# Attention stage: r loaded two tokens to a partition and spread by ScalarE, r's scaling and the conversion's clamp given new places in the step

## The chip, the cores and the metric

The kernel runs on one core of a Trainium2 chip. The metric is the device time of one execution in microseconds (us), lower is better. Before the change it is 455.89 us, the median of three runs that lie between 454.84 and 456.10 us.

## The reference

Three layers follow each other. Every array of the attention layer is float32; the last layer's arrays are float64.

```python
# r, k, v: [4, 8, 768, 48]; w, u: [8, 48]
state = np.zeros((B, H, D, D), dtype=np.float32)
for t in range(S):
    kt, vt, rt = (k[:, :, t], v[:, :, t], r[:, :, t])
    cur = np.einsum('bhd,bhe->bhde', u[None] * kt, vt)
    y[:, :, t] = np.einsum('bhd,bhde->bhe', rt, state + cur)
    state = w[None, :, :, None] * state + np.einsum('bhd,bhe->bhde', kt, vt)
...
# x = y as [3072, 384]; a soft mixture of 8 experts with 4 slots each
logits = x @ phi
...
# w_in: [384, 2048], w_out: [2048, 384], both float64
h = x @ w_in
g = np.where(h > 0.0, h, alpha * (np.exp(np.minimum(h, 0.0)) - 1.0))
return (g @ w_out).astype(np.float32)
```

## The kernel before

The attention layer is done in chunks of 128 tokens: 4 sequences of 6 chunks, 24 chunks in all, and one pass of the loop `for s in range(-2, NCH)` (lines 857 and after) is called a step here. A step works on several chunks at once, so that each engine has something of a later chunk to do while another chunk is waiting. In step s the kernel finishes the output rows of chunk s, makes the masked scores of chunk s + 1, and prepares r and k of chunk s + 2.

For a chunk these things happen:

- `load_r`, `load_k`, `load_v` (lines 502 to 514) bring 128 tokens of 8 heads, one token to a partition; a contiguous run in memory is one head's 48 floats, 192 bytes.
- `scale` (L517) multiplies k by powers of w on VectorE and writes `km`, whose heads are padded to 64 columns. r is loaded straight into the padded tiles `rp`.
- `turn(0, n)` transposes r: four transposes on TensorE into the PSUM tile `ps_r` (L522), then VectorE scales it by powers of w into `rT` (L532). `turn(1, n)` does the same for k: `ps_k` (L522), a copy by ScalarE into `kT` (L527), and the product r x k by VectorE, `qd` (L529).
- `update` (`pu`, L541), `scores` (`ps_a`, L554, one PSUM tile for the even and one for the odd heads), `causal` (`am`, L559: the mask on VectorE, one instruction for each of the two tiles), `bonus_a`, `bonus_c`, `bonus_b` (`ps_b`, `bt`, `ps_c`, `bs`, and `bv` on GpSimd, L601), `state` and `state_b` (`t1`, `qc` on GpSimd, `qb` on ScalarE).
- `before` (`py`, L612) starts the output of a chunk from the state, `rows_a` (`py`, L625) adds the scores' part, `rows_b` (`x`, L635) adds the bonus on VectorE and so empties the one PSUM tile `py`. `x_T` transposes the finished rows (`ps_x`, L644) and ScalarE copies them to `xT` (L646).

`ps_r`, `ps_x` and `ps_k` share a PSUM pool of two buffers (tag "pt"), so each of them waits until a buffer's readers are done. The pool chooses the buffer when the program is built.

Beside this, each of the first 20 steps converts a piece of the last layer's float64 weights into float32 ("wide"): two operations on ScalarE (`wide_a`, L313 and L314), a clamp (`wide_b1`, L317), a shift with a mask (`wide_b2`, L322), `wide_b3` (L328) and `wide_c` (L333) on VectorE, and in the following step `wide_d` on GpSimd (L336 and L337). They all work in place on the tile `scr`, in the order a, b1, b2, b3, c, d.

The order on each engine is written by hand: the program runs under `manual_schedule`, engines take their instructions in the order of the Python calls, and semaphores alone decide when each starts. All loads are issued from SyncE's queue, in the order of the calls. After the attention layer come the experts and then the last layer (from about 205 us on); the change touches neither.

Of the kernel before, what the change touches and what calls it, by code (L numbers as in the profile page):

```python
# [8 lines left out]
F32 = mybir.dt.float32  # L9
# [4 lines left out]
ALU = mybir.AluOpType  # L14
# [222 lines left out]
def kernel(  # L237
# [14 lines left out]
    nc = tc.nc  # L252
    B, H, S, D = r.shape
# [4 lines left out]
    C = 128  # L258
# [138 lines left out]
    with ExitStack() as actx:  # L397
# [28 lines left out]
        def tables():  # L426
            nc.vector.tensor_scalar(
                out=wd, in0=w_raw, scalar1=W_LO, scalar2=W_HI, op0=ALU.max, op1=ALU.min
            )

            nc.vector.memset(pw[:, 0, :, 0:1], 1.0)
            nc.vector.tensor_copy(out=pw[:, 0, :, 1:2], in_=wd.unsqueeze(2))
            n = 2
            while n <= 64:
                m = min(n - 1, 65 - n)
                nc.vector.tensor_tensor(
                    out=pw[:, 0, :, n:n + m], in0=pw[:, 0, :, 1:1 + m],
                    in1=pw[:, 0, :, n - 1:n].to_broadcast([128, HP, m]), op=ALU.mult,
                )
                n += m  # L440
            nc.vector.reciprocal(out=ri[:, :, 0:8], in_=pw[:, 0, :, 0:8])
            nc.vector.reciprocal(out=ri[:, :, 8:17], in_=pw[:, 0, :, 0:65:8])
            nc.vector.tensor_tensor(
                out=pw[:, 1, :, 0:64].rearrange("p h (b a) -> p h b a", a=8),
                in0=ri[:, :, 8:16].unsqueeze(3).to_broadcast([128, HP, 8, 8]),
                in1=ri[:, :, 0:8].unsqueeze(2).to_broadcast([128, HP, 8, 8]), op=ALU.mult,
            )
            nc.vector.tensor_copy(out=pw[:, 1, :, 64:65], in_=ri[:, :, 16:17])

            nc.vector.tensor_tensor(  # L450
                out=vt[:, :, 0:64], in0=pw[:, 0, :, 0:64], in1=pw[:, 1, :, 64:65].to_broadcast([128, HP, 64]),
                op=ALU.mult,
            )
            nc.scalar.copy(out=vt[:, :, 64:128], in_=pw[:, 0, :, 0:64])
            nc.vector.tensor_tensor(
                out=vk[:, :, 0:64], in0=pw[:, 1, :, 0:64], in1=pw[:, 0, :, 63:64].to_broadcast([128, HP, 64]),
                op=ALU.mult,
            )
            nc.scalar.copy(out=vk[:, :, 64:128], in_=pw[:, 1, :, 1:65])
            ps = pt_p.tile([128, 512], F32, tag="pt", name="ps_wk")  # L460
            for p in range(HP):
                nc.tensor.transpose(out=ps[:, 128 * p:128 * p + 128], in_=vk[:, p, 0:128], identity=ident)
            nc.scalar.copy(out=wk, in_=ps.rearrange("p (h d) -> p h d", d=64)[:, :, 0:D])
# [25 lines left out]
                    out=i3[32 * g:32 * g + 32, :], in_=ident[32 * g:32 * g + 32, 32 * g:32 * g + 32]  # L489
                )  # L490

        rp = [ae2.tile([128, H, 64], F32, name=f"rp{i}", bufs=1) for i in range(2)]
        km = ae1.tile([128, H, 64], F32, name="km")
        kT = ae1.tile([128, HP, 128], F32, name="kT")
        qb = [at1.tile([128, HP, 2, D], F32, name=f"qb{i}") for i in range(2)]
        t1 = at1.tile([128, HP, D], F32, name="t1")
        qc = at1.tile([128, HP, D], F32, name="qc")

        rk, vd, rT, qd, am, bsb, xs, xT, misc = {}, {}, {}, {}, {}, {}, {}, {}, {}


        def load_r(n):
            b, c = divmod(n, NC)
            nc.sync.dma_start(out=rp[n % 2][:, :, 0:D], in_=r[b, :, C * c:C * c + C, :].rearrange("h p d -> p h d"))

        def load_k(n):
            b, c = divmod(n, NC)
# [8 lines left out]
        def scale(n):  # L516
            nc.vector.tensor_tensor(out=km[:, :, 0:D], in0=rk.pop(n), in1=wk, op=ALU.mult)  # L517

        def turn(i, n):
            ps = pt_p.tile([128, HP, 128], F32, tag="pt", name=f"ps_{'rk'[i]}")  # L520
            for p in range(HP):
                nc.tensor.transpose(  # L522
                    out=ps[:, p, :], in_=(km if i else rp[n % 2])[:, 2 * p:2 * p + 2, :].rearrange("p a d -> p (a d)"),
                    identity=ident,
                )
            if i:
                nc.scalar.copy(out=kT, in_=ps)  # L527
                qd[n] = at2.tile([128, HP, 128], F32, tag="qd", name="qd", bufs=1)
                nc.vector.tensor_tensor(out=qd[n], in0=rT[n], in1=ps, op=ALU.mult)  # L529
            else:  # L530
                rT[n] = at2.tile([128, HP, 128], F32, tag="rT", name="rT", bufs=2)
                nc.vector.tensor_tensor(out=rT[n], in0=ps, in1=vt, op=ALU.mult)  # L532


        pu = pu_p.tile([128, HP, D], F32, name="pu")
        nc.vector.memset(pu, 0.0)
# [16 lines left out]
                q = slice(64 * a, 64 * a + 64)  # L553
                nc.tensor.matmul(out=aps[a][:, p, :], lhsT=kT[q, p, :], rhs=rT[n][q, p, :], start=True, stop=True)  # L554

        def causal(n):
            for a in range(2):
                am[n, a] = at2.tile([128, HP, 128], F32, tag="am", name="am", bufs=3)
                nc.vector.tensor_tensor(  # L559
                    out=am[n, a], in0=aps[a], in1=mask.unsqueeze(1).to_broadcast([128, HP, 128]), op=ALU.mult  # L560
                )

        def bonus_a(n):
            pb = pm_p.tile([128, 512], F32, tag="pm", name="ps_b")
# [20 lines left out]
        def state_b(n):  # L585
            if n % NC < NC - 1:
                for a in range(2):
                    s = slice(64 * a, 64 * a + 64)
                    nc.scalar.copy(out=qb[(n + 1) % 2][s, :, a, :], in_=qc[s])
# [223 lines left out]
        def wide(j, f):  # L813
            if 0 <= j < NP:
                raw, a = piece(j)
                if f is not wide_d:
                    f(raw, a)
                    return
                merged = []
                for o, at, i, c, p, m in spans(j):  # L820
                    if merged and merged[-1][0] == o:
                        merged[-1][3] += m
                    else:
                        merged.append([o, at, p, m])
                for o, at, p, m in merged:
                    wide_d(raw[:, at:at + m, :], a[:, at:at + m], (wov if o else wiv)[:, p:p + m])
# [2 lines left out]
        load_k(0)  # L829
        load_v(0)  # L830
        nc.scalar.dma_start(out=phi_sb, in_=phi.rearrange("(k p) c -> p k c", p=128))
        for t in (*rp, km):
            nc.gpsimd.memset(t[:, :, D:], 0.0)
        nc.gpsimd.memset(uw, 0.0)
        for i in range(2):
# [3 lines left out]
        nc.scalar.activation(out=wf, in_=wf, func=ACTF.Exp)  # L839
        warm(12)  # L840
        tables()
        load_r(1)
        load_k(1)
        load_v(1)
# [9 lines left out]
        for s in range(-2, NCH):  # L854
# [26 lines left out]
            if now:  # L881
                for p in range(HP):
                    rows_a(s, p)
                rows_b(s)
                wide(s, wide_b1)
                wide(s - 1, wide_d)
                if s >= 1 and s + 2 < NP:
                    wide_load(s + 2)
            if nxt:
                for p in range(HP):  # L890
                    scores(s + 1, p)
                causal(s + 1)
                bonus_a(s + 1)
                bonus_c(s + 1)
            if not last:
                extra()
            if ahead:
                turn(0, s + 2)
            if 2 <= s + 4 < NCH:
                load_r(s + 4)  # L900
            if nxt:
                for p in range(HP):
                    before(s + 1, p)
# [3 lines left out]
                logits(GS - 1, G - 1, G)  # L907
            if nxt:
                bonus_b(s + 1)
            wide(s, wide_b2)  # L910
            if ahead:
                turn(1, s + 2)
            wide(s, wide_b3)
            wide(s, wide_c)
            if nxt:
                state_b(s + 1)
            if s == NCH - 2:
                warm(3)
            extra()
# [502 lines left out]
```

## Time and profile before

| | before |
|---|---|
| time, median of 3 runs | 455.89 us |
| the profiled execution's own time | 454.1 us |
| its span, first to last instruction | 452.4 us |
| TensorE busy | 414.1 us, 92% |
| TensorE weight loads busy | 361.4 us, 80% |
| VectorE busy | 369.3 us, 82% |
| ScalarE busy | 262.2 us, 58% |
| GpSimd busy | 157.2 us, 35% |
| granted TensorE clock, mean | 0.995 of full speed |
| loads of r (`rp`) | 24 of 192 KB |

The shares are means over the whole span, and the kernel has stages with different limits. The change lies in the first 170 us, so it is read from the views of that stretch: busy time by windows, waits, and the timelines of single steps.

### The profile page before, as it was taken

To read this page: it belongs to the slowest core of one execution; us is meant where nothing else is said; L and a number is where in the kernel's file an instruction comes from. 1 tells how busy PE (TensorE), PEld (TensorE's weight loads), DVE (VectorE), ACT (ScalarE), POOL (GpSimd) and SP (SyncE) were. 2 spreads that over 40 slices of the span, in tenths; PEclk is the share of its full clock that TensorE was granted. 3 is DMA by queue.
4 is the path that set the end of the run, shared out by engine and by line. 5 is a ranking of instruction groups with operands and counts; after the bars stand their busy time and mean duration, and the time that the engine had idled before them with its cause. 6 is when DMAs were issued, how large, how long until landed. Compare 5 with 4: busy or idle time off the path is not lost.

```text
span 452.4 us, 10086 instructions
## 1 busy us (share of the span) xinstructions
PE 414.1 (92%) x4021; PEld 361.4 (80%) x4021; DVE 369.3 (82%) x581; ACT 262.2 (58%) x482; POOL 157.2 (35%) x170
## 2 busy tenths in 40 slices
PE   6988988898988989997999999998999899999995
PEld 5876776776776874455999999996989889999994
DVE  5899989899898744768889999995989889768661
ACT  2543453545453332337787878874777768776750
POOL 2355455456446413500003333350213135423340
PEclk9999999999999999999999999998999999999999
DMA  8979799999999968940001111111111002011212
GB/s 124 227 163 268 191 258 265 266 282 186 269 266 260 278 212 280 313 175 1 0 1 35 36 35 38 35 36 35 36 35 35 1 0 72 35 54 52 71 71 76
DMA packets 97575, 57.41 MB, mean 127 GB/s; under 512 B 77808, under 2 KB 89328, under 8 KB 97520
## 3 DMA queue, kind: packets, MB, share of 16 engines
q1 hardware_dynamic: 96704, 56.64, 46.0%
q8 instruction: 33, 0.54, 0.5%
q14 instruction: 22, 0.18, 0.1%
q10 hardware_dynamic: 816, 0.05, 0.1%
HBM read 51.96 MB, written 4.72 MB: 125 GB/s over the span
## 4 chain that ended last, share of the span: by engine, by line
PE 54%; DVE 24%; issue 9%; ACT 7%; DMA 3%; SPq 1%; POOL 1%; DVEq 0%; ACTq 0%; POOLq 0%
PE fo L1261 10%; PE fo L1264 10%; PE fo L1262 10%; DVE ex L1235 4%; DVE ex L1230 4%; PE fh L1216 3%; PE py L612 3%; PE ps_k L522 3%; PE ps_a L554 2%; PE pd L1029 2%; PE ph L1007 2%; DVE am L559 2%; PE py L625 2%; DVE km L517 2%; DVE scr L317 2%
## 5 line engine op out<-in xcount | busy, mean ns | idle before, releaser
L1261 PE MATMUL fo<-wh,gh 128*128 128x384 f32 x384 | 130.8, 341 | 3.8 <-ACT acc L1198 2.7
L1262 PE MATMUL fo<-wl,gh 128*128 128x384 f32 x384 | 130.1, 339 | 0.0
L1264 PE MATMUL fo<-wh,gl 128*128 128x384 f32 x384 | 125.9, 340 | 3.3 <-DVE gl L1246 3.3
L1230 DVE SCALAR_TENSOR_TENSOR ex<-ex,th 128x1024 f32<-128x1024 f32 (+1 forms) x52 | 60.9, 1172 | 23.8 <-ACT ex L1227 23.6
L1261 PEld LDWEIGHTS fo<-wh,gh 128*128 128x128 f32 x384 | 72.5, 189 | 8.6 <-ACT acc L1198 4.3
L1264 PEld LDWEIGHTS fo<-wh,gl 128*128 128x128 f32 x384 | 72.0, 188 | 4.2 <-DVE gl L1246 4.2
L1262 PEld LDWEIGHTS fo<-wl,gh 128*128 128x128 f32 x384 | 72.4, 189 | 1.9
L1224 ACT ACTIVATE th<-fh 128x1024 f32<-128x1024 f32 (+1 forms) x53 | 50.4, 951 | 38.0 <-PE fh L1216 38.0
L1246 DVE TENSOR_TENSOR gl<-ex,gh 128x1024 fp32r<-128x1024 f32 (+1 forms) x52 | 68.3, 1314 | 1.7 <-ACT gh L1243 1.3
L336 POOL TENSOR_TENSOR cv<-raw,cv 128x384 f32<-128x384 f32 x12 | 19.4, 1620 | 136.5 <-ACT gh L1243 51.5
L1235 DVE SCALAR_TENSOR_TENSOR ex<-ex,fh 128x1024 f32<-128x1024 f32 (+1 forms) x52 | 58.8, 1131 | 0.5 <-ACT ex L1227 0.4
L1227 ACT ACTIVATE ex<-fh 128x1024 f32<-128x1024 f32 (+1 forms) x53 | 50.3, 949 | 9.7 <-DVE gl L1246 9.5
L1243 ACT CAST gh<-ex 128x1024 fp32r<-128x1024 f32 (+1 forms) x52 | 51.4, 988 | 6.2 <-DVE ex L1235 4.9
L1203 POOL TENSOR_TENSOR acc<-os,acc 128x384 f32<-128x384 f32 x20 | 26.7, 1346 | 44.0 <-ACT os L1202 44.0
L646 ACT COPY xT<-ps_x 128x384 f32<-128x384 f32 x24 | 11.5, 479 | 43.2 <-PE ps_x L644 43.2
L583 POOL TENSOR_TENSOR qc<-t,w 128x192 f32<-128x192 f32 x20 | 14.5, 725 | 59.7 <-DVE t L582 21.8
L1216 PE MATMUL fh<-cT,mst 128*128 128x512 f32 x96 | 31.1, 404 | 1.9 <-DVE mst L1144 1.1
L559 DVE TENSOR_TENSOR am<-ps_a,mask 128x512 f32<-128x512 f32 x48 | 30.7, 678 | 0.2 <-PE ps_a L554 0.2
L529 DVE TENSOR_TENSOR qd<-rT,ps_k 128x512 f32<-128x512 f32 x24 | 16.5, 686 | 15.3 <-ACT kT L527 15.3
L554 PE MATMUL ps_a<-rT,kT 64*128 64x128 f32 x384 | 27.9, 285 | 0.3 <-ACT kT L527 0.2
L522 PE MATMUL ps_k<-ident,km 128*128 128x128 f32 x96 | 15.6, 285 | 12.4 <-ACT xT L646 6.4
L625 PE MATMUL py<-vd,am 128*64 128x48 f32 x768 | 26.5, 222 | 0.0
(161 smaller groups left out, 695.0 us busy)
## 6 DMA issues: line engine op xcount, KB each, us to landing
we<-in_moe_w_dram SPq DMA_DIRECT2D x14, 768.0 KB, 8.0
we<-in_moe_w_dram SPq DMA_DIRECT2D x16, 512.0 KB, 6.2
rp<-in_r_dram SPq DMA_DIRECT2D x24, 192.0 KB, 4.6
rk<-in_k_dram SPq DMA_DIRECT2D x24, 192.0 KB, 4.6
vd<-in_v_dram SPq DMA_DIRECT2D x24, 192.0 KB, 4.8
out_dram<-acc SPq DMA_DIRECT2D x24, 192.0 KB, 1.9
we<-in_moe_w_dram SPq DMA_DIRECT2D x16, 256.0 KB, 5.4
scr<-in_moe_w_out_dram SPq DMA_DIRECT2D x10, 384.0 KB, 5.7
```

The costliest lines, as they stand in the source:

```text
L554: nc.tensor.matmul(out=aps[a][:, p, :], lhsT=kT[q, p, :], rhs=rT[n][q, p, :], start=True, stop=True)
L559: nc.vector.tensor_tensor(out=am[n, a], in0=aps[a], in1=mask.unsqueeze(1).to_broadcast([128, HP, 128]), op=ALU.mult)
L1216: nc.tensor.matmul(out=ph[n][:, i, :], lhsT=mst[(f + i) // 8][:, 128 * ((f + i) % 8):128 * ((f + i) % 8) + 128], rhs=cT[:, TB * blk:TB * b ...
L1224: nc.scalar.activation(out=th[n][:, s], in_=ph[n][:, s], func=ACTF.Tanh, scale=0.5)
L1227: nc.scalar.activation(out=ex[n][:, s], in_=ph[n][:, s], func=ACTF.Exp)
L1230: nc.vector.scalar_tensor_tensor(out=ex[n][:, s], in0=ex[n][:, s], scalar=1.0, in1=th[n][:, s], op0=ALU.add, op1=ALU.mult)
L1235: nc.vector.scalar_tensor_tensor(out=ex[n][:, s], in0=ex[n][:, s], scalar=0.0, in1=ph[n][:, s], op0=ALU.min, op1=ALU.max)
L1243: nc.scalar.copy(out=gh[n][:, s], in_=ex[n][:, s])
L1246: nc.vector.tensor_tensor(out=gl[n][:, s], in0=ex[n][:, s], in1=gh[n][:, s].bitcast(F32), op=ALU.subtract)
L1261: nc.tensor.matmul(out=o, lhsT=gh[n][:, i, s], rhs=wh, start=(f == first), stop=False)
L1262: nc.tensor.matmul(out=o, lhsT=gh[n][:, i, s], rhs=wl, start=False, stop=False)
L1264: nc.tensor.matmul(out=o, lhsT=gl[n][:, i, s], rhs=wh, start=False, stop=(f == final))
```

## The change

r is loaded for two chunks at once into `rw`, with two consecutive tokens to a partition, so that a contiguous run is 384 bytes; there are 12 such loads. `spread` copies on ScalarE the even or the odd tokens of such a pair of chunks into the padded tile `rp`, one copy for each chunk's worth of tokens. `turn_r` transposes them as before, but its scaled result goes to every second column of a tile `rT` for both chunks, so that both halves must have been turned before the first of the two chunks can be used. For that, `turn_r` runs one step earlier than `turn(0, ...)` did; two spreads and one `turn_r` stand ahead of the loop, and the second of these spreads goes into the memory of `kT` (`k0`), since `rp` is one tile now.

Inside a step, `turn_r` with r's scaling stands between the two masking instructions, the clamp b1 goes from behind `x` to just ahead of r x k, and the shift b2 goes behind r x k.

```diff
+            spread(0)
+            spread(1, k0)
             ps = pt_p.tile([128, 512], F32, tag="pt", name="ps_wk")
...
-        rp = [ae2.tile([128, H, 64], F32, name=f"rp{i}", bufs=1) for i in range(2)]
+        rw = [ae2.tile([128, H, 2, D], F32, name=f"rw{i}", bufs=1) for i in range(2)]
+        rp = ae2.tile([128, H, 64], F32, name="rp", bufs=1)
...
-        def load_r(n):
-            b, c = divmod(n, NC)
-            nc.sync.dma_start(out=rp[n % 2][:, :, 0:D], in_=r[b, :, C * c:C * c + C, :].rearrange("h p d -> p h d"))
+        def load_r(g):
+            b, c = divmod(2 * g, NC)
+            nc.sync.dma_start(
+                out=rw[g % 2].rearrange("p h j d -> p h (j d)"),
+                in_=r[b, :, C * c:C * c + 2 * C, :].rearrange("h (p j) d -> p h (j d)", j=2),
+            )
+
+        def spread(i, dst=rp):
+            if i < NCH:
+                nc.scalar.copy(out=dst[:, :, 0:D], in_=rw[i // 2 % 2][:, :, i % 2, :])
...
+        def turn_r(i, src=rp):
+            if i >= NCH:
+                return
+            ps = flip(src, "ps_r")
+            g, j = divmod(i, 2)
+            if j == 0:
+                rg[g] = at2.tile([128, HP, 2 * C], F32, tag="rT", name="rT", bufs=2)
+                for c in range(2):
+                    rT[2 * g + c] = rg[g][:, :, C * c:C * c + C]
+            nc.vector.tensor_tensor(
+                out=rg[g].rearrange("p h (c u j) -> p h c u j", c=2, j=2)[:, :, :, :, j],
+                in0=ps.rearrange("p h (c u) -> p h c u", c=2),
+                in1=vt.rearrange("p h (u j) -> p h u j", j=2)[:, :, :, j].unsqueeze(2).to_broadcast([128, HP, 2, 64]),
+                op=ALU.mult,
+            )
...
         tables()
+        turn_r(0)
         load_r(1)
...
                 rows_b(s)
-                wide(s, wide_b1)
                 wide(s - 1, wide_d)
...
-                causal(s + 1)
+                causal(s + 1, 0)
                 bonus_a(s + 1)
                 bonus_c(s + 1)
             if not last:
                 extra()
-            if ahead:
-                turn(0, s + 2)
-            if 2 <= s + 4 < NCH:
-                load_r(s + 4)
+            turn_r(s + 3, k0 if s == -2 else rp)
+            if nxt:
+                causal(s + 1, 1)
+            if s % 2 == 0 and s // 2 + 3 < NCH // 2:
+                load_r(s // 2 + 3)
...
+            wide(s, wide_b1)
+            if ahead:
+                turn_k(s + 2)
             wide(s, wide_b2)
-            if ahead:
-                turn(1, s + 2)
             wide(s, wide_b3)
             wide(s, wide_c)
             if nxt:
                 state_b(s + 1)
+            spread(s + 4)
```

`flip` holds the four transposes, and `turn_k` is what `turn(1, ...)` was.

In the program as built, VectorE's part of a step reads so before (a middle step, from the output rows `x` to the end of the conversion):

```order
L635 TENSOR_TENSOR x<-py,bv 128x384
L317 TENSOR_SCALAR scr<-scr 128x384
L559 TENSOR_TENSOR am<-ps_a,mask 128x512 x2
L532 TENSOR_TENSOR rT<-ps_r,vt 128x512
L322 TENSOR_SCALAR scr<-scr 128x384
L529 TENSOR_TENSOR qd<-rT,ps_k 128x512
L328 SCALAR_TENSOR_TENSOR scr<-scr 128x384
L333 TENSOR_SCALAR scr<-scr 128x384
```

and so after the change, in the same step:

```order
L658 TENSOR_TENSOR x<-py,bv 128x384
L582 TENSOR_TENSOR am<-ps_a,mask 128x512
L546 TENSOR_TENSOR rT<-ps_r,vt 128x512
L582 TENSOR_TENSOR am<-ps_a,mask 128x512
L317 TENSOR_SCALAR scr<-scr 128x384
L557 TENSOR_TENSOR qd<-rT,ps_k 128x512
L322 TENSOR_SCALAR scr<-scr 128x384
L328 SCALAR_TENSOR_TENSOR scr<-scr 128x384
L333 TENSOR_SCALAR scr<-scr 128x384
```

r's scaling has two instructions ahead of it instead of four; the clamp (L317) stands where the shift (L322) stood, and the shift is behind `qd`.

On TensorE the order within a step is the same, but what the transposes of k wait for is not. Before, in a middle step (the names in brackets are the semaphores of the engines waited for; Activation is ScalarE):

```order
L612 MATMUL py<-qb_147,rT 128x96 [waits DVE_49,Activation_49]
L612 MATMUL py<-qb_147,rT 128x96 x3
L644 MATMUL ps_x<-ident,x 128x128 x3
L594 MATMUL ps_c<-ident,bt 128x128 [waits Activation_49]
L522 MATMUL ps_k<-ident,km 128x128 [waits Activation_49]
```

and after:

```order
L635 MATMUL py<-qb_148,rT 128x96 [waits DVE_49]
L635 MATMUL py<-qb_148,rT 128x96 x3
L667 MATMUL ps_x<-ident,x 128x128 x3
L617 MATMUL ps_c<-ident,bt 128x128 [waits Activation_49]
L532 MATMUL ps_k<-ident,km 128x128 [waits DVE_49]
```

The first transpose of k waited for ScalarE and now waits for VectorE.

At the start, VectorE goes from the last table to the first k (`km`) like this before:

```order
L455 TENSOR_TENSOR vk<-pw 128x4x64
L466 TENSOR_TENSOR w_141<-pw 128x4
L469 TENSOR_TENSOR uw<-ud,wd 64x4 x2
L517 TENSOR_TENSOR km<-rk_155,wk 128x8x48
L532 TENSOR_TENSOR rT<-ps_r,vt 128x512
```

and after:

```order
L455 TENSOR_TENSOR vk<-pw 128x4x64
L546 TENSOR_TENSOR rT<-ps_r,vt 128x512
L468 TENSOR_TENSOR w_141<-pw 128x4
L471 TENSOR_TENSOR uw<-ud,wd 64x4 x2
L527 TENSOR_TENSOR km<-rk_156,wk 128x8x48
L546 TENSOR_TENSOR rT<-ps_r,vt 128x512
```

A scaling of r, which needs r's first transposes, stands ahead of the small tables and of `km`.

## Rows read from the trace of the kernel before

**Rows 1.** Busy time by windows: window, us, PE, PEld, DVE, ACT, POOL, clock, DMA share.

```profile
80.00:90.00 10.00, 8.61 (x167) 7.26 (x162) 9.22 (x19) 5.33 (x17) 3.58 (x5) 1.00 1.02 284
```

**Rows 2.** Waits between 15 and 169 us: total us, times, longest.

```profile
PE ps_k L522 <- ACT xT L646: 6.4, 14, 0.5
PE ps_k L522 <- DVE rT L532: 5.2, 6, 1.3
```

**Rows 3.** VectorE's timeline, two steps: start, us, what, [idle before <- releaser].

```profile
76.38 0.55 DVE L635 TENSOR_TENSOR x<-py,bv 128x384 f32<-128x384 f32 x1
76.85 0.34 DVE L317 TENSOR_SCALAR scr<-scr 128x384 f32<-128x384 f32 x1
77.12 1.28 DVE L559 TENSOR_TENSOR am<-ps_a,mask 128x512 f32<-128x512 f32 x2
...
80.44 0.69 DVE L529 TENSOR_TENSOR qd<-rT,ps_k 128x512 f32<-128x512 f32 x1 [1.06 <-ACT kT L527]
...
83.43 0.54 DVE L635 TENSOR_TENSOR x<-py,bv 128x384 f32<-128x384 f32 x1
83.90 0.70 DVE L317 TENSOR_SCALAR scr<-scr 128x384 f32<-128x384 f32 x1
...
87.49 0.69 DVE L529 TENSOR_TENSOR qd<-rT,ps_k 128x512 f32<-128x512 f32 x1 [0.23 <-ACT kT L527]
```

**Rows 4.** TensorE's timeline in the first of these two steps.

```profile
78.34 0.27 PE L594 MATMUL ps_c<-ident,bt 128*128 128x128 f32 x1
79.08 0.66 PE L522 MATMUL ps_k<-ident,km 128*128 128x128 f32 x4 [0.46 <-ACT xT L646]
```

**Rows 5.** ScalarE's timeline in that step.

```profile
78.54 0.48 ACT L646 COPY xT<-ps_x 128x384 f32<-128x384 f32 x1 [2.46 <-PE ps_x L644]
78.92 0.17 ACT L596 COPY bs<-ps_c 128x8 f32<-128x8 f32 x1
79.82 0.59 ACT L527 COPY kT<-ps_k 128x512 f32<-128x512 f32 x1 [0.73 <-PE ps_k L522]
```

**Rows 6.** TensorE's timeline in step 20, at 151 to 157 us.

```profile
153.25 0.27 PE L594 MATMUL ps_c<-ident,bt 128*128 128x128 f32 x1
153.42 0.66 PE L522 MATMUL ps_k<-ident,km 128*128 128x128 f32 x4
```

**Rows 7.** VectorE's timeline in the step from 68.65 us.

```profile
68.65 0.56 DVE L635 TENSOR_TENSOR x<-py,bv 128x384 f32<-128x384 f32 x1
69.12 1.19 DVE L317 TENSOR_SCALAR scr<-scr 128x384 f32<-128x384 f32 x1
...
73.52 0.69 DVE L529 TENSOR_TENSOR qd<-rT,ps_k 128x512 f32<-128x512 f32 x1 [0.78 <-ACT kT L527]
```

**Rows 8.** TensorE's timeline in the same step.

```profile
70.88 0.27 PE L594 MATMUL ps_c<-ident,bt 128*128 128x128 f32 x1
72.16 0.66 PE L522 MATMUL ps_k<-ident,km 128*128 128x128 f32 x4 [1.01 <-DVE rT L532]
```

**Rows 9.** GpSimd's timeline in the same step.

```profile
69.07 1.02 POOL L336 TENSOR_TENSOR scr<-scr 128x384 f32<-128x384 f32 x1
70.17 1.02 POOL L337 TENSOR_TENSOR win<-scr 128x384 f32<-128x384 f32 x1
71.70 0.83 POOL L601 TENSOR_TENSOR bv<-vd,bs 128x384 f32<-128x384 f32 x1 [0.51 <-ACT bs L596]
```

**Rows 10.** Groups by line and form, first 170 us: busy us, mean ns, idle before.

```profile
L532 DVE TENSOR_TENSOR rT<-ps_r,vt 128x512 f32<-128x512 f32 x24 | 16.3, 678 | 0.0
...
L328 DVE SCALAR_TENSOR_TENSOR scr<-scr 128x384 int32<-128x384 int32 x20 | 11.0, 552 | 0.0
```

**Rows 11.** VectorE's timeline at the start.

```profile
8.76 0.56 DVE L517 TENSOR_TENSOR km<-rk,wk 128x384 f32<-128x384 f32 x1 [0.98 <-ACT wk L463]
```

**Rows 12.** ScalarE's timeline at the start.

```profile
8.25 0.48 ACT L463 COPY wk<-ps_wk 128x384 f32<-128x384 f32 x1 [1.17 <-PE ps_wk L462]
```

**Rows 13.** TensorE's timeline at the start.

```profile
8.05 0.60 PE L522 MATMUL ps_r<-ident,rp 128*128 128x128 f32 x4
```

More of the change, by code (lines that the diff above doesn't have):

```diff
@@ L497 @@
         qc = at1.tile([128, HP, D], F32, name="qc")
-        rk, vd, rT, qd, am, bsb, xs, xT, misc = {}, {}, {}, {}, {}, {}, {}, {}, {}
-        def load_r(n):
-            b, c = divmod(n, NC)
-            nc.sync.dma_start(out=rp[n % 2][:, :, 0:D], in_=r[b, :, C * c:C * c + C, :].rearrange("h p d -> p h d"))
+        rk, vd, rT, rg, qd, am, bsb, xs, xT, misc = {}, {}, {}, {}, {}, {}, {}, {}, {}, {}
+        def load_r(g):
[7 more added lines that the diff above has]
+                nc.scalar.copy(out=dst[:, :, 0:D], in_=rw[i // 2 % 2][:, :, i % 2, :])
         def load_k(n):
@@ L517, in scale, with flip, turn_k @@
             nc.vector.tensor_tensor(out=km[:, :, 0:D], in0=rk.pop(n), in1=wk, op=ALU.mult)
-        def turn(i, n):
-            ps = pt_p.tile([128, HP, 128], F32, tag="pt", name=f"ps_{'rk'[i]}")
+        def flip(src, name):
+            ps = pt_p.tile([128, HP, 128], F32, tag="pt", name=name)
             for p in range(HP):
                 nc.tensor.transpose(
-                    out=ps[:, p, :], in_=(km if i else rp[n % 2])[:, 2 * p:2 * p + 2, :].rearrange("p a d -> p (a d)"),
-                    identity=ident,
-                )
[L526 to L532, printed above, removed]
+                    out=ps[:, p, :], in_=src[:, 2 * p:2 * p + 2, :].rearrange("p a d -> p (a d)"), identity=ident
+                )
+            return ps
+        def turn_r(i, src=rp):
[13 more added lines that the diff above has]
+            )
+        def turn_k(n):
+            ps = flip(km, "ps_k")
+            nc.scalar.copy(out=kT, in_=ps)
+            qd[n] = at2.tile([128, HP, 128], F32, tag="qd", name="qd", bufs=1)
+            nc.vector.tensor_tensor(out=qd[n], in0=rT[n], in1=ps, op=ALU.mult)
         pu = pu_p.tile([128, HP, D], F32, name="pu")
@@ L554, in scores, with causal @@
                 nc.tensor.matmul(out=aps[a][:, p, :], lhsT=kT[q, p, :], rhs=rT[n][q, p, :], start=True, stop=True)
[L556 to L561, printed above, removed]
+        def causal(n, a):
+            am[n, a] = at2.tile([128, HP, 128], F32, tag="am", name="am", bufs=3)
+            nc.vector.tensor_tensor(
+                out=am[n, a], in0=aps[a], in1=mask.unsqueeze(1).to_broadcast([128, HP, 128]), op=ALU.mult
+            )
         def bonus_a(n):
@@ L831 @@
         nc.scalar.dma_start(out=phi_sb, in_=phi.rearrange("(k p) c -> p k c", p=128))
-        for t in (*rp, km):
+        k0 = kT.rearrange("p a (b d) -> p (a b) d", b=2)
+        for t in (rp, km, k0):
             nc.gpsimd.memset(t[:, :, D:], 0.0)
```

## The prediction

> **What bounds the kernel now.** The windows come first: between 80 and 90 us VectorE is busy 9.22 of 10 us, TensorE 8.61 [rows 1]. That looks like a stage that VectorE bounds, and the reader should distrust it, because a busy engine may be spending time that a wait would have taken anyway. The waits say what kind of wait: TensorE's transposes of k (`ps_k`) wait 14 times for the copy `xT` (6.4 us, 0.46 each) and 6 times for r's scaling `rT` (5.2 us) [rows 2].
>
> The timeline of single steps settles it. I count a step from one `x` to the next. In the step from 76.38 the clamp L317 takes 0.34 us and VectorE then idles 1.06 us before `qd`, which starts 4.06 us after `x`. In the step from 83.43 the clamp takes 0.70 and the idle time is only 0.23, yet `qd` starts at 87.49, again 4.06 after `x` [rows 3]. So in a plain step VectorE's slow instructions are paid out of a wait. The cycle that sets the step is: `x` empties the one `py` tile, TensorE writes the next `py` and transposes `x`, ScalarE copies `xT`, only then `ps_k`, then `kT`, then `qd`; behind `qd` VectorE does L328, L333, small work, `km`, and the next `x`. On TensorE the transpose `ps_c` starts at 78.34 and ends at 78.61, but `ps_k` starts at 79.08, held by `xT` [rows 4], which ends at 79.02 [rows 5].
>
> A second kind of step is late. From 68.65 the clamp takes 1.19 us [rows 7], beside GpSimd's addition and multiplication L336 and L337 [rows 9]; `rT` slides behind it, `ps_k` waits 1.01 us for `rT` and starts at 72.16 [rows 8], and `qd` starts at 73.52, 4.87 after `x` [rows 7]. From the same timeline over all steps I count, among the 20 steps with a conversion, 11 plain ones, 4 late ones, 3 that open a sequence (no `py` from the state, so `qd` is early), and the first and third, which hold extra set-up work.
>
> **The change part by part.**
>
> *r's scaling earlier.* It now follows `x` and one masking instruction. `x` takes a slot of 0.47 and a masking instruction 0.64 (half of 1.28) [rows 3], and with 0.68 for itself [rows 10] `rT` is done about 1.8 us after `x`. The built program shows that `ps_k` now waits for VectorE and no longer for ScalarE. At 1.8 us `rT` is no hindrance, since `ps_c` starts only 1.96 after `x` [rows 3, 4]. In step 20, where `rT` was early already, `ps_k` follows the start of `ps_c` by 0.17 [rows 6]. A plain step then has `ps_k` at 78.51 instead of 79.08: 0.57 earlier. ScalarE is free for `kT` (`bs` ends at 79.09, `ps_k` would end at 79.17) [rows 5], so `kT` and `qd` follow by the same 0.57. Gain in 11 plain steps: 6.3 us. In the late step `ps_k` goes from 72.16 to 71.05, a gain of 1.1 [rows 8]; four of them: 4.4 us.
>
> *The second mask later.* `am` of the odd heads is read only in the next step; VectorE reaches it at once. Nothing.
>
> *The clamp into the gap.* VectorE is through with the second mask about 2.4 us after `x` and `qd` comes at 3.5; the clamp of 0.34 fits. Without that cover it would cost its 0.34, with GpSimd in the way up to 1.19 [rows 7].
>
> *The shift behind `qd`.* This is the price. The shift was in the gap; now it stands in the tail from `qd` to the next `x`. No row shows it there; it has the size of the clamp, 0.34, and L328 must wait for its result, so I take 0.39, between 0.34 and the 0.70 of a clamp that meets GpSimd [rows 3]. I take the low end because GpSimd's last operation, `bv`, ends 3.88 after `x` [rows 9], before `qd` is through. In 11 plain and 4 late steps: 5.9 us.
>
> *The odd store of `rT`.* It now writes every second column. L328 reads and writes every second word and takes 552 ns for 384 columns [rows 10], the rate of 678 for 512, so I take 678. The other end, half the rate, is a rival below.
>
> *`spread`.* 24 copies of 384 columns on ScalarE, 0.48 us each by the copy `wk` of the same size [rows 12]. It stands last in a step, and ScalarE idles 2.46 us ahead of `xT` [rows 5]: covered. Were it not, 24 x 0.48 = 11.5 us would be due.
>
> *The loads.* 24 loads become 12 of twice the size and half as many packets per byte. In this stretch the DMA engines are 1.02 busy [rows 1], but no wait of rows 2 is for a load, so I put this at nothing; each pair is issued two steps and more before its first spread.
>
> *The sequence openers.* There `qd` gains somewhat less than half a microsecond and pays 0.39: -0.1 each, -0.3 in all. The first and third step: nothing.
>
> *The start.* A scaling of r and the small tables now stand ahead of `km`. r's first transposes end at 8.65 [rows 13]; then 0.6 for the scaling and 0.43 for the tables put `km` at 9.7 instead of 8.76 [rows 11]. The two spreads ahead of `wk` take 0.96 and fit into the 1.17 us that ScalarE idles there [rows 12]. Cost: 0.95, between 0 and 1.7 (a second scaling in the path as well).
>
> *The end.* r's last transposes (0.66) leave the last steps, in which TensorE runs without a gap: -0.3, between 0 and -0.66.
>
> Sum: -6.3 - 4.4 + 5.9 - 0.3 + 0.95 - 0.3 = -4.45 us. The profiled execution took 454.1 us, so it would take 449.7; it stood 1.8 below the median of the runs shown. On the median, 455.9 - 4.4 = **451.5 us**. With the shift at 0.5 and the start at 1.7 it is 454; with nothing lost at the start and the shift partly hidden it is 449.
>
> **Rivals.**
>
> *The copy still ends last (slower).* If `ps_k`, or `kT` behind it, still comes only when `xT` is done, the shift's 0.39 is paid for nothing: 11 x 0.39 = 4.3; the late steps fall to plain ones, 0.81 - 0.39 = 0.42 each, -1.7; the openers +0.6; start and end +0.65. That is +3.9, 459.8 us. It decides where `rT` ends later than 2.7 us after `x`. For it: ScalarE gets more work in front of `xT`. Against: what `ps_k` waits for in the built program. Chance 0.10.
>
> *The clamp is caught by GpSimd (slower).* Seen in the trace: the clamp that starts 0.05 us after L336 [rows 7, 9] ends only 0.22 after it. In its new place the clamp comes at about 2.4 us, while L337 may run and just ahead of `bv`. If `bv` goes first, the clamp ends when the held shift did in the step from 83.43, 0.23 us before 87.49, or 3.83 after `x` [rows 3], and `qd` follows. Plain steps: -0.2 + 0.39, 11 x 0.19 = 2.1; late ones `qd` at 4.1, -0.38 each, -1.5; openers +0.6; start and end +0.65. That is +1.85, 457.7 us. It decides where the clamp is still waiting when `bs` ends. The Trainium skill (*Advanced Engine Details and Errata*, VectorE Performance Modes, Mode Summary) has this rule: VectorE's second port is shared with GpSimd, and two-port VectorE instructions and GpSimd's block each other. By that rule alone the clamp loses in its new place too; the trace agrees that it can be held, 1.19 us against 0.34. Against the rival: in the late step the clamp was served between L336 and L337, so the port is given in turn, and L337 ends half a microsecond before `bv` starts [rows 9]. Chance 0.14.
>
> *The strided store runs at half rate.* `rT` then takes 678 + 512 ns, and `ps_k` loses some 0.2 of its 0.57: plain steps +0.02 each, late ones -0.5 each, start +1.5, end and openers -0.6. About -0.9, 455.0 us. Chance 0.10.
>
> The remaining 0.02 is for what I have not thought of.
>
> **How the numbers follow.** The forecast has 0.64. Faster and slower mean by more than 0.3%, 1.4 us, about what a measurement of this kernel can tell. The forecast gives 0.62 faster and 0.02 same; the strided store 0.04 faster, 0.06 same; the caught clamp 0.05 same and 0.09 slower; the copy 0.10 slower, and 0.01 each for same and slower. Faster 0.66, same 0.14, slower 0.20. The range of the forecast alone is 449 to 454. The whole one is 448.8 to 457.5: it takes in the strided store and nearly half of the caught clamp and leaves out the copy and the rest, a little under 2 in 10.
>
> **What would show it.** After the change a plain step should have `ps_k` about 0.17 us behind `ps_c`, with no wait for `xT`; `qd` 3.5 us after `x`; the clamp at 0.34 to 0.5 in every step; the shift at 0.34 behind `qd`; no `ps_k` waiting a microsecond for `rT`; a step of 6.2 to 6.5 us; the first `km` near 9.7. I am wrong if `qd` still starts 4 us after `x`, if the clamp ends after `bv`, if `rT` takes over a microsecond, or if TensorE waits for `spread` ahead of `ps_r`.

## The result and the profile after

The changed kernel takes 447.28 us (median of four runs, 446.97 to 448.24); the kernel before took 456.0 us beside it (454.84 to 456.31). The ratio is 0.983 with an interval of 0.980 to 0.986. The medians thus differ by 8.7 us. In the profiled executions it is 447.44 against 454.1, so 6.7 us less; a later comparison gave 447.54 against 454.64, 7.1 us less.

The predicted time was 451.5 and the range 448.8 to 457.5: the direction was right, the size was not, and the time lies 1.5 us below the range.

Busy time by windows of the kernel after, in the stretch that stood for the stage before [rows 1], same columns:

```profile
80.00:90.00 10.00, 8.31 (x131) 6.48 (x131) 8.99 (x18) 5.43 (x17) 5.85 (x7) 1.00 1.04 312
```

Read alone, this row shows nothing of the change: VectorE is still busy nine tenths of the time and the DMA engines still all of it (1.04; the view's share can come out a little above 1). The waits between 15 and 166 us do (total us, times, longest):

```profile
DVE qd L557 <- ACT kT L555: 14.8, 21, 1.7
...
PE ps_k L532 <- DVE rT L546: 1.0, 3, 0.3
...
PE ps_k L532 <- ACT xT L669: 0.5, 1, 0.5
```

TensorE's transposes of k waited 14 times for `xT` and 6 times for `rT` [rows 2]; now it is once and three times, 1.5 us in place of 11.6. What is left is the chain itself: `ps_k`, then `kT`, then `qd` waiting for `kT`.

VectorE's timeline after, a late step (from 67.43) and a plain one (from 74.25), the same two steps of the program as in [rows 7] and the first of [rows 3]. The `x` at 80.95 opens the next step:

```profile
67.43 0.55 DVE L658 TENSOR_TENSOR x<-py,bv 128x384 f32<-128x384 f32 x1
67.90 0.68 DVE L582 TENSOR_TENSOR am<-ps_a,mask 128x512 f32<-128x512 f32 x1
68.58 0.69 DVE L546 TENSOR_TENSOR rT<-ps_r,vt 128x512 f32<-128x512 f32 x1
...
69.79 0.40 DVE L317 TENSOR_SCALAR scr<-scr 128x384 f32<-128x384 f32 x1
70.99 0.69 DVE L557 TENSOR_TENSOR qd<-rT,ps_k 128x512 f32<-128x512 f32 x1 [0.81 <-ACT kT L555]
71.60 0.35 DVE L322 TENSOR_SCALAR scr<-scr 128x384 int32<-128x384 int32 x1
...
74.25 0.54 DVE L658 TENSOR_TENSOR x<-py,bv 128x384 f32<-128x384 f32 x1
...
76.51 0.48 DVE L317 TENSOR_SCALAR scr<-scr 128x384 f32<-128x384 f32 x1
77.56 0.69 DVE L557 TENSOR_TENSOR qd<-rT,ps_k 128x512 f32<-128x512 f32 x1 [0.57 <-ACT kT L555]
...
80.95 0.55 DVE L658 TENSOR_TENSOR x<-py,bv 128x384 f32<-128x384 f32 x1
```

In the plain step `qd` starts 3.31 us after `x`, where it was 4.06; in the late one 3.56, where it was 4.87. The clamp L317 takes 0.48 and 0.40 and stands in VectorE's gap ahead of `qd`; the shift L322 takes 0.35 behind it. TensorE and ScalarE in the plain step:

```profile
76.14 0.27 PE L617 MATMUL ps_c<-ident,bt 128*128 128x128 f32 x1
76.25 0.60 PE L532 MATMUL ps_k<-ident,km 128*128 128x128 f32 x4
```

```profile
76.34 0.48 ACT L669 COPY xT<-ps_x 128x384 f32<-128x384 f32 x1 [2.79 <-PE ps_x L667]
76.72 0.17 ACT L619 COPY bs<-ps_c 128x8 f32<-128x8 f32 x1
76.94 0.59 ACT L555 COPY kT<-ps_k 128x512 f32<-128x512 f32 x1
```

`ps_k` starts 0.11 us behind `ps_c`, before `xT` has even begun, where it stood 0.74 behind it and idle [rows 4]. `kT` now starts straight behind `bs`, where ScalarE had to wait 0.73 us for `ps_k` [rows 5]. The groups by line and form of the first 163 us (busy us, mean ns, idle before):

```profile
L546 DVE TENSOR_TENSOR rT<-ps_r,vt 128x512 f32<-128x512 f32 x24 | 16.4, 684 | 1.5 <-ACT wk L465 1.3
...
L317 DVE TENSOR_SCALAR scr<-scr 128x384 f32<-128x384 f32 x20 | 8.5, 427 | 0.0
...
L322 DVE TENSOR_SCALAR scr<-scr 128x384 int32<-128x384 int32 x20 | 7.1, 353 | 0.0
```

The store into every second column costs nothing (684 ns against 678 [rows 10]). The start, on VectorE and on ScalarE:

```profile
8.69 0.69 DVE L546 TENSOR_TENSOR rT<-ps_r,vt 128x512 f32<-128x512 f32 x1 [1.30 <-ACT wk L465]
...
9.75 0.56 DVE L527 TENSOR_TENSOR km<-rk,wk 128x384 f32<-128x384 f32 x1
```

```profile
8.20 0.48 ACT L465 COPY wk<-ps_wk 128x384 f32<-128x384 f32 x1 [0.34 <-PE ps_wk L464]
```

`wk` comes at 8.20, not later than before [rows 12], so the two spreads ahead of it are hidden; `km` is 0.99 later [rows 11].

Summed over the steps of the two traces, from `x` to the next `x`, the profiled 6.7 us come out so: 11 plain steps -3.8 (-0.34 each), the 4 late ones -4.0 (-0.90 to -1.14), the 3 openers +0.1, the first and third +0.1, the last two -0.6; the first `x` comes 1.07 later, and what follows the last `x` takes 0.4 more.

### The profile page after: what moved, and what is told of

It reads as the page before. It is cut to its first block, busy times and chain, and to the rows that moved or that the text cites. A ratio compares the mean times of both kernels' runs of the same rounds, so it can differ in the third digit from the quotient of the medians.

```text
span 445.7 us, 10074 instructions
## 1 busy us (share of the span) xinstructions
PE 414.5 (93%) x4021; PEld 364.1 (82%) x4021; DVE 359.3 (81%) x581; ACT 271.3 (61%) x506; POOL 155.2 (35%) x170
## 4 chain that ended last, share of the span: by engine, by line
PE 64%; DVE 17%; ACT 8%; issue 7%; DMA 2%; SPq 1%; POOL 0%; ACTq 0%; DVEq 0%
PE fo L1288 12%; PE fo L1291 12%; PE fo L1289 12%; PE fh L1243 4%; PE py L635 4%; PE ps_a L578 3%; PE py L648 3%; DVE ex L1262 2%; PE pd L1056 2%; PE ph L1034 2%; DVE ex L1257 2%; DMA rw<-in_r_dram 2%; DVE km L527 2%; DVE scr L328 1%; PE ps_x L667 1%
## 5 line engine op out<-in xcount | busy, mean ns | idle before, releaser
L336 POOL TENSOR_TENSOR cv<-raw,cv 128x384 f32<-128x384 f32 x12 | 19.4, 1617 | 137.8 <-ACT gh L1270 52.2
L582 DVE TENSOR_TENSOR am<-ps_a,mask 128x512 f32<-128x512 f32 x48 | 32.4, 679 | 0.6 <-PE ps_a L578 0.6
L635 PE MATMUL py<-qb,rT 128*128 128x96 f32 x160 | 22.1, 281 | 6.7 <-DVE x L658 6.7
```

## The experiments

Three parts can be taken apart: r's scaling between the masks, the clamp and shift round r x k, and the loads with `spread`. The first four runs are compared with one set of runs of the kernel before (median 454.3 us), the next four with another (454.64), the last three with a third (454.51).

**r's scaling alone** (before, and only this):

```diff
-                causal(s + 1)
+                causal(s + 1, 0)
 ...
                 turn(0, s + 2)
+            if nxt:
+                causal(s + 1, 1)
```

> The kernel before, with r's scaling moved between the two masking instructions and nothing else; loads and conversion as before. Theory A (release: the gain comes from r's scaling ending early, so that the transposes of k wait for it and no longer for the copy xT): the late steps lose about 0.6 us each and the steps whose clamp is not held lose about 0.5, while in steps with a held clamp r's scaling still ends at 2.9 us after x; together -3 to -5 us, 451 to 453 us. Rival B (loads: half or more of the gain comes from r's larger runs in memory): -1 us or less, 455 to 456. Rival C (port: the gain comes from the clamp no longer colliding with GpSimd): 455 to 456, the clamp's mean stays near 0.85 us.

Measured: 451.99 us, ratio 0.992 (0.989 to 0.995). VectorE's timeline, a step with a held clamp and one with a free clamp:

```profile
63.06 0.55 DVE L634 TENSOR_TENSOR x<-py,bv 128x384 f32<-128x384 f32 x1
63.52 1.17 DVE L317 TENSOR_SCALAR scr<-scr 128x384 f32<-128x384 f32 x1
...
65.22 0.68 DVE L532 TENSOR_TENSOR rT<-ps_r,vt 128x512 f32<-128x512 f32 x1
...
67.31 0.69 DVE L529 TENSOR_TENSOR qd<-rT,ps_k 128x512 f32<-128x512 f32 x1 [0.43 <-ACT kT L527]
...
76.81 0.55 DVE L634 TENSOR_TENSOR x<-py,bv 128x384 f32<-128x384 f32 x1
77.27 0.35 DVE L317 TENSOR_SCALAR scr<-scr 128x384 f32<-128x384 f32 x1
78.14 0.68 DVE L532 TENSOR_TENSOR rT<-ps_r,vt 128x512 f32<-128x512 f32 x1
...
80.24 0.69 DVE L529 TENSOR_TENSOR qd<-rT,ps_k 128x512 f32<-128x512 f32 x1 [0.42 <-ACT kT L527]
```

Where the clamp is free, `qd` comes 3.43 after `x`: nearly the whole gain. Where the clamp runs beside GpSimd's L336 (63.47 to 64.48), `rT` stands behind 1.17 us of clamp, and `qd` comes at 4.25. The waits of this run say the same: `xT` is gone as a cause (once), and `rT` is the new one:

```profile
PE ps_k L522 <- DVE rT L532: 8.0, 13, 1.3
```

The start of this profiled run is disturbed: TensorE's granted clock is 0.76 between 8 and 11 us and 0.50 between 11 and 13, where it is 1.00 in the trace of before, and the first `x` comes at 16.74 instead of 15.49. From the first `x` to the last the run is 3.7 us shorter than before.

**The clamp and the shift alone** (before, and only this):

```diff
-                wide(s, wide_b1)
 ...
-            wide(s, wide_b2)
+            wide(s, wide_b1)
             if ahead:
                 turn(1, s + 2)
+            wide(s, wide_b2)
```

> The kernel before, with the clamp moved to just ahead of r x k and the shift behind it, nothing else. Theory A: the transposes of k still wait for xT in most steps, r x k still starts 4.06 us after x in a plain step, and the shift is paid at 0.39 us in 11 of them (+4.3), the four late steps gain 0.4 each (-1.6): +2 to +4 us, 458 to 460 us. Rival B: 456, no change. Rival C: the held clamps go away, 0.5 us in each of 20 steps would be won: -4 us or more, 452 or less.

Measured: 457.23 us, ratio 1.0054 (1.0038 to 1.0069): slower. The clamps take 0.34 to 0.49, yet the waits hold the same line as before [rows 2]:

```profile
PE ps_k L522 <- ACT xT L646: 6.4, 14, 0.5
```

`qd` stays 4.06 after `x`, and the shift behind it makes a plain step 6.82 in place of 6.42: 0.40, the price that the prediction had put at 0.39. A faster clamp buys nothing in a step in which `xT` ends last. In the four late steps, where `rT` ended last, it does: they are 0.7 us shorter each, the shift paid. From the first `x` to the last the run is 1.9 us longer than before.

**Both moves, with the old loads** (before with the two edits above together):

> The kernel before with both changes of order (r's scaling between the masks, clamp ahead of and shift behind r x k), r loaded as before. Theory A: the steps are as short as after the whole change to within 0.1 us (6.1 to 6.2 us plain), and the start does not pay its 1.07 us: 447 to 449 us, as fast as the whole change or up to 1 us off it. Rival B: clearly slower than the whole change, 451 us or more. Rival C: like A in time, but then the clamp alone must give most of it.

Measured: 449.63 us (448.48 to 452.51), ratio 0.990 (0.987 to 0.994). Alone the two parts gave -0.8% and +0.5%; together they give -1.0%. The second removes what the first ran into. A plain step takes 6.14, `qd` at 3.38. But the step from 86.30 us on takes 6.96 and the next one, from 93.26, takes 9.39, where the same two take 6.51 and 6.35 in the trace after. TensorE's timeline there:

```profile
88.20 0.66 PE L522 MATMUL ps_k<-ident,km 128*128 128x128 f32 x4 [0.35 <-DVE rT L532]
91.45 0.56 PE L541 MATMUL pu<-vd,km 128*48 128x48 f32 x16 [2.59 <-DMA vd<-in_v_dram]
...
93.08 2.08 PE L554 MATMUL ps_a<-rT,kT 64*128 64x128 f32 x16
```

TensorE waits 2.59 us for a load of v; in the trace of before the only such wait is 0.6, on the side of TensorE's weight loads (PEld):

```profile
PEld ps_r L522 <- DMA vd<-in_v_dram: 0.6, 1, 0.6
```

The windows of that stretch (us, PE, PEld, DVE, ACT, POOL, clock, DMA share, GB/s):

```profile
85.00:88.00 3.00, 2.75 (x32) 1.49 (x28) 2.96 (x8) 0.73 (x3) 1.92 (x3) 1.00 1.05 356
88.00:91.00 3.00, 0.66 (x4) 0.42 (x4) 2.45 (x6) 1.50 (x5) 1.73 (x2) 1.00 0.85 211
91.00:94.00 3.00, 2.55 (x56) 2.46 (x58) 2.48 (x7) 1.00 (x2) 1.37 (x2) 0.76 1.02 193
94.00:97.00 3.00, 3.00 (x43) 2.49 (x41) 0.69 (x1) 0.27 (x1) 1.31 (x2) 0.67 0.96 241
```

The DMA engines were about full, as they were before [rows 1], up to 90 us; but between 90 and 91 us, the last microsecond of TensorE's wait, their share is 0.41, so a lack of bandwidth alone does not account for the whole wait. After the idle stretch TensorE's granted clock is 0.76 and 0.67, means over stretches that are partly at its lower level, 1.2 GHz, and `ps_a` takes 2.08 in place of the 1.16 it takes in the trace after.

Without the 3.5 us that these two steps lose, the run would be 7.1 us shorter than before from the first `x` to the last, where the two parts alone give -3.7 and +1.9. That is how much the one depends on the other.

**The loads, with the old order inside the step** (the whole change, its order put back):

```diff
                 rows_b(s)
+                wide(s, wide_b1)
 ...
                 causal(s + 1, 0)
+                causal(s + 1, 1)
 ...
-            if nxt:
-                causal(s + 1, 1)
 ...
-            wide(s, wide_b1)
+            wide(s, wide_b2)
             if ahead:
                 turn_k(s + 2)
-            wide(s, wide_b2)
```

> The whole change with the order inside a step put back (both masks, then r's scaling; clamp behind x, shift ahead of r x k): r is loaded two tokens to a partition, spread, and scaled one step earlier. Theory A: start +1 us, steps as before but for up to 0.1 us each: 455 to 457.5 us. Rival B: most of the gain is here, 451 us or less. Rival C: 455 to 457, since the clamp collides as before.

Measured: 456.28 us, ratio 1.0042 (1.0027 to 1.0057). A plain step is 6.36, 0.06 less than before, and the first `x` comes at 18.17 instead of 15.49, which is not earned back. Not all of this late start belongs to the loads: with the same loads the first `x` comes at 16.56 in the trace after, and in this profiled run TensorE's granted clock is 0.76 between 11 and 13 us and 0.50 between 13 and 15, where it is 1.00 in the trace after. One of the openers (step 17) takes 7.72 in place of 6.48, since its `ps_k` waits 1.9 us for `rT`. So alone the loads gain nothing; how much of the 2.0 us is their own loss and how much the clock's is not shown.

**The whole change again**, as the control of the next runs:

> The whole change, unchanged, as the measure for the runs beside it on the same chip: 0.980 to 0.986 of the kernel before; plain steps of 6.08 us, start to the first x 16.6 us.

Measured: 447.54 us, ratio 0.985 (0.983 to 0.987). All waits of TensorE for v in this stretch come to half a microsecond.

**The whole change, with r's bytes in runs of 192 again:**

```diff
-            nc.sync.dma_start(
-                out=rw[g % 2].rearrange("p h j d -> p h (j d)"),
-                in_=r[...].rearrange("h (p j) d -> p h (j d)", j=2),
-            )
+            for j in range(2):
+                nc.sync.dma_start(
+                    out=rw[g % 2][:, :, j, :],
+                    in_=r[...].rearrange("h (p j) d -> p h j d", j=2)[:, :, j, :],
+                )
```

> The whole change, but each pair of chunks of r is loaded by two transfers with one token's 192 bytes to a run, so the same bytes go to the same places at about the same time with twice the packets. Theory D (packets: in the shorter step the transfers have become the thing that is nearly late, and r's larger runs keep them ahead): steps with a wait of TensorE for v or of ScalarE for a converted piece, as in the change of order alone; 1 to 4 us slower than the whole change. Rival E (lead: what keeps the whole change free of such waits is that r is issued earlier and in another place of the queue): within 0.7 us of the whole change. Theory A without D expects E's number too.

Measured: 450.2 us, ratio 0.990 (0.988 to 0.992), so 2.7 us worse than the whole change beside it. The same instructions run on the four compute engines; the packets are shorter, and SyncE issues r's loads as 24 again. The page's line of DMA packets, after:

```profile
DMA packets 85095, 57.41 MB, mean 129 GB/s; under 512 B 65328, under 2 KB 76848, under 8 KB 85040
```

and with the short runs, with two of its waits:

```profile
DMA packets 97575, 57.41 MB, mean 128 GB/s; under 512 B 77808, under 2 KB 89328, under 8 KB 97520
...
PE pu L566 <- DMA vd<-in_v_dram: 4.2, 6, 1.6
ACT scr L313 <- DMA scr<-in_moe_w_out_dram: 3.4, 3, 2.0
```

The stalls sit in four steps (12, 14, 17, 19), which together take 2.9 us longer than the same four after. This is where half as many packets are worth their time: not before the change, whose steps leave the transfers time enough, but in the shorter steps. In the trace after a packet of 192 bytes takes 15 ns (median) and one of 384 takes 22, not 30. The number of transfers changed together with the packets, and no run takes the two apart: between 15 and 155 us SyncE spends 118 us on issuing transfers with the short runs and 93 after, and the v whose wait ends at 91.18 us is issued 1.2 us later than after and lands 7.9 us after its issue instead of 5.8.

**The shift ahead of r x k** (the whole change, and only this):

```diff
             wide(s, wide_b1)
+            wide(s, wide_b2)
             if ahead:
                 turn_k(s + 2)
-            wide(s, wide_b2)
```

> The whole change with the shift put back ahead of r x k, right behind the clamp. Rival F (the gap of 0.6 us that VectorE has ahead of r x k takes the shift in): the tail loses 0.39 us in some 18 steps, -5 to -7 us against the whole change. Theory G (port: the shift comes when GpSimd has begun bv and is held until bv ends, 3.6 us after x, so r x k starts at 3.8 and not at 3.3): +0.1 us a step, the whole change to 3 us slower, the shift's mean 0.7 us or more instead of 0.35.

Measured: 445.25 us (442.65 to 447.89), ratio 0.979 (0.976 to 0.982). Of the 15 plain and late steps, 8 have a held shift, as theory G expected, and 7 a free one, as rival F did. VectorE's timeline, a held shift and a free one:

```profile
72.58 0.55 DVE L658 TENSOR_TENSOR x<-py,bv 128x384 f32<-128x384 f32 x1
...
75.35 0.99 DVE L322 TENSOR_SCALAR scr<-scr 128x384 int32<-128x384 int32 x1
76.26 0.68 DVE L557 TENSOR_TENSOR qd<-rT,ps_k 128x512 f32<-128x512 f32 x1
...
79.25 0.55 DVE L658 TENSOR_TENSOR x<-py,bv 128x384 f32<-128x384 f32 x1
...
81.89 0.36 DVE L322 TENSOR_SCALAR scr<-scr 128x384 int32<-128x384 int32 x1
82.56 0.69 DVE L557 TENSOR_TENSOR qd<-rT,ps_k 128x512 f32<-128x512 f32 x1 [0.32 <-ACT kT L555]
```

GpSimd's `bv` starts at 75.30, 0.05 ahead of the held shift. Held, `qd` comes at 3.68 and the step is nearly as long as after (-0.03); free, the step is 0.4 shorter. TensorE also waits 3.0 us for v in this profiled run, 2.2 of it at one time, so a part of the gain is lost in a stall.

**The first scaling of r behind the first `km`** (the whole change, and only this: `turn_r(0)` goes from ahead of the loop to behind the first `km`):

```diff
-        turn_r(0)
 ...
                 scale(s + 2)
+            if s == -2:
+                turn_r(0)
```

> The whole change with the first scaling of r issued behind the first k instead of ahead of it. The start pays 1.07 us to the first x; the first k would start near 8.7 again, its transposes wait for the scaling that now follows it, so half of the loss comes back: -0.3 to -0.9 us against the whole change, first x at 15.7 to 16.3 us. If the loss is due to the loads or the spreads instead: no change, 16.6 us.

Measured: 445.99 us, ratio 0.980 (0.979 to 0.982). The first `x` comes at 16.09 in place of 16.56, as it should. The time fell by 1.5, three times that; the last section tells where the rest comes from.

**Both of these together** (the two edits above):

> The whole change with two further moves: the shift ahead of r x k, and the first scaling of r behind the first km. Alone they gave 445.25 and 445.99 against 447.5 of the change. Theory G (a step is set by the chain through VectorE, and the transfers keep up with a little to spare): the gains add, about 2.2 and 1.5 us, 443.8 to 444.6. Theory H (the transfers set the pace already: shorter steps are paid back as waits for v): the second gain is lost, 445.0 to 446.0, and the profile has TensorE waiting 3 us or more for vd between 85 and 135 us.

Measured: 444.65 us, ratio 0.979 (0.977 to 0.981): at the slow edge of what adding gains should give, and below what a pace set by transfers should give. TensorE's waits for v come to 0.9 us. The ratio is not told apart from that of the shift alone.

**Both, with v loaded one step earlier** into a fifth buffer:

```diff
-            vd[n] = at2.tile([128, H, D], F32, tag="vd", name="vd", bufs=4)
+            vd[n] = at2.tile([128, H, D], F32, tag="vd", name="vd", bufs=5)
 ...
-            if 2 <= s + 3 < NCH:
-                load_v(s + 3)
+            if 2 <= s + 4 < NCH:
+                load_v(s + 4)
```

> The kernel with both moves, and v loaded one step earlier into a fifth buffer. If the waits for v come from a burst (a transfer queued behind a weight's block), one step of 6 us more in hand takes them away: no wait for vd over 0.5 us, and 1 to 2 us less than the kernel with both moves, 442.5 to 443.5. If the transfers are short of bandwidth over the whole stretch, the wait only goes elsewhere (to scr on ScalarE, or to r or k), and the time is that of the kernel with both moves within 0.7 us.

Measured: 444.17 us (442.07 to 448.5), ratio 0.978 (0.974 to 0.982). The waits for v are gone, and ScalarE waits longer for the weights' pieces, 1.5 us where the kernel with both moves has 0.6:

```profile
ACT scr L313 <- DMA scr<-in_moe_w_out_dram: 1.5, 2, 0.8
```

That is what the reading by bandwidth expected: the lateness moves to another transfer. The times span 6 us, so they do not settle it.

**Both, with the blocks of w1 spread over 21 steps instead of 20:**

```diff
-            if s >= 2 and (s - 2) * (NWE - 1) // NP >= nwe and nwe < NWE - 1:
+            if s >= 2 and (s - 2) * (NWE - 1) // (NP + 1) >= nwe and nwe < NWE - 1:
```

> The kernel with both moves, and the blocks of w1 spread over 21 steps of the attention instead of 20 (three of them, after steps 11, 18 and 20, go out a step later). If the stall in step 12 comes from the block issued just ahead of it, it goes or moves by one or two steps: then 0.5 to 1.5 us less, or the same time with the stall after step 13. If bandwidth over the whole stretch is short, the same bytes later cost the attention less and the stages behind it more: within 0.7 us of the kernel with both moves.

Measured: 444.17 us, ratio 0.976 (0.973 to 0.978); TensorE waits 3.4 us for v in the profiled run, the slowest of the five (445.86), and the longest stall holds up step 12. There it stood with the shift alone (7.64 us for that step) and with the start alone (7.16), but the profile of the kernel with both moves has none there (6.32). So the stall comes and goes from run to run or kernel to kernel, and one profile of each does not show whether the block just ahead causes it. The intervals of the last three overlap, so none of them is shown to be the better; by the ratio to the kernel before, taken on another chip, each beats the whole change by about 0.6 to 0.9%.

## Why the prediction was wrong

**The mechanism held.** `ps_k` follows `ps_c` by 0.11 (predicted 0.17), `qd` comes 3.3 after `x` (3.5), `rT` is done 1.74 after `x` (1.8), all 20 clamps take 0.34 to 0.50, the shift takes 0.35, the step 6.08 (6.2 to 6.5), the first `km` comes at 9.75 (9.7). Taken one at a time, the parts show why: `ps_k` is let go by the scaling between the masks, but only if the clamp is out of its way.

**No rival came.** The copy `xT` holds `ps_k` once. The strided store runs at full rate. The clamp was held for no longer than some 0.15 us. The rule of the Trainium skill that the prediction weighed (*Advanced Engine Details and Errata*, VectorE Performance Modes, Mode Summary) is nonetheless borne out where an instruction does run beside GpSimd's: 1.17 for the clamp that alone takes 0.35, 0.99 for the shift that alone takes 0.36. That the clamp escaped was partly luck. In the plain step shown it runs from 76.51 to 76.99, while GpSimd's L337 ends at 76.77 and `bv` starts at 76.96: it slips in between the two. The shift right behind it does not, as the run with the shift ahead of r x k shows.

**What failed, by the steps of the prediction.** The profiled runs gave 6.7 us where the sum had 4.45. Of the 2.2 missing, the plain steps hold 1.8 and the late ones 1.15; small terms of both signs take 0.7 back (the openers gave +0.1 and not -0.3, and what follows the last `x` took 0.4 more, which the sum did not have).

*"A plain step then has ps_k at 78.51 instead of 79.08: 0.57 earlier."* This term was sized too small. The start of `ps_k` moved by 0.68 and `qd` by 0.74. Of that, the order alone, with the old loads, gives `ps_k` 0.62, since it follows `ps_c` by 0.11 and not by 0.17; `kT` gains 0.06 more, since it starts 0.69 after `ps_k` instead of 0.75; and the step is 6.14 (-0.28). The remaining 0.06 came with the new loads, in which TensorE's `py` starts 0.60 instead of 0.69 after `x`. In the built program it then waits for VectorE alone, with the old loads for ScalarE's `qb` as well, though that ends some 2 us ahead of `x`; that the second wait costs the time is not shown. The tail cost 0.40, as predicted. So a plain step gained 0.34 and not 0.18: 1.8 us over eleven.

*"In the late step ps_k goes from 72.16 to 71.05, a gain of 1.1 [...]; four of them."* I took one late step for all four. In it `ps_k` comes 2.25 after `x`, and 1.24 is gained. Two of the other three have their `ps_c` as early as a plain step, 1.96 and not 2.22 after `x`, and there `ps_k` gained 1.36 and 1.48. The four steps gave -4.0 and not -2.8.

*"The loads [...] no wait of rows 2 is for a load, so I put this at nothing."* The number stands, since the change ran almost without stalls (0.3 us for v), but the reason fell. (The rows shown have no such wait; the trace of before has one of 0.6.) The near absence of waits showed slack only for the steps as they were. With the DMA engines 1.02 busy [rows 1], shorter steps ask for the same bytes sooner, and with r loaded in short runs again 2.7 us of the gain went into stalls (450.2). The larger runs were thus a part of the gain, and not a thing beside it; the sum never asked. The Trainium skill (*DMA: Bandwidth & Descriptors*, Specifications) puts the least transfer at line rate at 512 bytes, so by its rule both lengths, 192 and 384, fall short of it. No run here brings r to that length; below it, the doubling brought the 22 ns in place of twice 15, and, with half the transfers, the 2.7 us.

*"On the median, 455.9 - 4.4 = 451.5."* I added a sum made against a profiled run of 454.1 to a median of three runs, 1.8 above it. In the three sets of runs of before that the experiments used, the medians were 454.3, 454.64 and 454.51, close to the profile. With the sum set on the profile the forecast would have been 449.65, still 2.2 slower than the profiled run after. The range, shifted with it by 1.8, would have begun at 447.0 and just held the measured time; that would have been luck, with the terms above still too small.

The terms that came right or near: the start, 1.07 against 0.95; the shift, 0.40 against 0.39; the spreads, hidden; the two last steps, -0.6 against -0.3.

## What to carry to other kernels

Two edits that each lose or win little alone can be one edit: a wait with two possible last arrivals is shortened only when both come early, so look for the second in line before pricing the first. A load that nobody waits for today is not free when the DMA engines are full: price it in the step length that the change will make, not in the present one. And set a sum on the run that it was read from, not on a median of other runs.

## What the runs showed that I had not expected

TensorE's clock takes its own share. Behind the attention layer, in a stretch that the change does not touch, windows of 4 us of the kernel after:

```profile
200.00:204.00 4.00, 1.90 (x8) 1.19 (x8) 3.67 (x7) 3.45 (x9) 0.00 (x0) 1.00 0.02 4
204.00:208.00 4.00, 3.96 (x13) 3.77 (x14) 3.84 (x7) 2.96 (x6) 0.00 (x0) 0.57 0.00 0
```

and the same stretch in the run with the first scaling of r moved:

```profile
200.00:204.00 4.00, 2.26 (x12) 1.30 (x8) 3.44 (x8) 3.45 (x9) 0.00 (x0) 1.00 0.02 4
204.00:208.00 4.00, 3.60 (x20) 3.43 (x20) 3.82 (x7) 2.95 (x7) 0.00 (x0) 1.00 0.00 0
```

TensorE is busy 1.90 us of four in the one and 2.26 in the other; then the granted clock has a mean of 0.57 in the one, partly at its lower level of 1.2 GHz, and stays at 1.00 in the other, and 13 matmuls are done where the other does 20. From the last `x` to the end the kernel after takes 284.6 us with two such falls (a second near 304 us), the kernel before 284.1 with one (in the window from 300 to 325, 0.93), the moved start 282.8 with none. So of that profiled run's 1.5 us less, the edit gave 0.5 at the start and the part behind the last `x`, which it does not touch, 1.8, and a stall for v in step 12 (7.16 us instead of 6.35) took 0.8 back. The clock shows between runs of one kernel, too: the 23 runs of before in the first set go from 452.84 us at a mean clock of 0.999 to 456.11 at 0.985, so the 1.8 us between a median and a profile of before are within what goes with it. The six runs with v loaded earlier go from 442.07 us at 0.996 to 448.5 at 0.985; whether that wide a span is the clock alone is not shown. What decides whether the clock falls after such a stretch, no run here settles.
